# Reordering maxima, attention results and the last gate's steps in a clustered-attention and expert-layer kernel

## Chip, cores and metric

The kernel runs on one core of one Trainium2 chip. The metric is the device time of one execution in microseconds (us). Engines are named as the profile does: PE (TensorE, matmuls), PEld (its weight loads), DVE (VectorE), ACT (ScalarE), POOL (GpSimd), SP (SyncE, which issues transfers).

## What is computed

Attention in which each query sees only the keys of its own cluster, for 2 batches of 8 heads, 768 positions, 64 features; its output, 1536 tokens of 512 features, goes through a layer of 8 experts, each token to the one with the highest logit.

```
q_assign = np.argmax(einsum(q_n, c_n)); k_assign = np.argmax(einsum(k_n, c_n))
scores = np.where(q_assign == k_assign, scale * q @ k.T, -1e9)
attn = softmax(scores); x = (attn @ v) as 1536 x 512
logits = x @ w_gate; expert_idx = np.argmax(logits, axis=1)
gate_w = softmax(logits)[expert_idx]
# tokens take places in their expert's rows in order, up to capacity
y = relu(disp @ w1) @ w2; out[i] = gate_w[i] * y[expert_idx[i], pos[i]]
```

## The kernel before

The 16 heads (two batches of eight) are passes i = 0 to 15. A pass has twelve groups g. A group issues two matmuls for a 128 x 384 block of masked scores (`st_group`, L414 and L415, tile s), whose exponentials ScalarE writes (pf, L419). Before a head's scores the row maxima must be known: a maximum is a matmul (`max_tile`, L351, tile m) that VectorE reduces (mx, L358). Maxima run ahead of the scores: `ahead` takes the next one from a list of twelve per head, one behind each group, two behind the groups in `TWICE`. After a head's last one `max_chain` joins the halves (mxx, L364), and two groups later `max_rows` turns them (mtp, L390) and sends them as a row.

`hooks(i, g)` puts the rest of the work behind certain groups. At g = 2 the second values batch of pass i - 1 (`pv_batch`, L443, tile o, values times exponentials, in tiles of 128 x 64), its strips (`sum_strips`, L469, tile rsp, row sums in tiles of 128 x 32), and the evictions. At g = 5 and 6 the row sums are turned (rtp, L487) and inverted (r, L493 to L495, three steps on VectorE). At g = 8 the first values batch of pass i. At g = 11 `out_stage` (L581, tile otp): three products of the unscaled result with an identity and the gate's weights, 128 x 144 each, which `out_scale` scales at g = 2 two passes on. Odd passes also assign the clusters of a coming pair of heads: `cl_assign` ends at g = 10 with the one-hot (ohb, L259), and the next pass turns it at g = 0 (ctb, L286).

The order of each engine is what the code says (`keep`): TensorE, VectorE, ScalarE and GpSimd run their lists in order. Two tiles of PSUM serve the maxima (psM), three the scores (psS), two small results (psT), one the values (psO). `opening` holds pass 0 and the step to pass 1.

The gate (`gate`, three calls: the first batch's six blocks of 128 tokens, then the second's first three, then its last three) finds each token's expert as a one-hot (goh), counts places with matmuls (gps, L656 to L662), makes row indices (gw, gsi) and scatters the tokens (L724). The last call runs beside the first expert's first tile, in whose matmuls its steps stand; the next token rows of expert 0 can be loaded only when its scatters have landed.

Of the kernel before, what the change touches and what calls it, by code (L numbers as in the profile page):

```python
# [7 lines left out]
F32 = mybir.dt.float32  # L8
R32 = mybir.dt.float32r
BF16 = mybir.dt.bfloat16  # L10
I32 = mybir.dt.int32
AF = mybir.ActivationFunctionType
ALU = mybir.AluOpType
AX = mybir.AxisListType
# [9 lines left out]
def kernel(  # L24
# [29 lines left out]
    WARM1 = 1  # L54
    WARM2 = 12
    WARM3 = 3
    G_B0, G_B1, G_TURN, G_OUT = 8, 2, 5, 11
    TWICE = {(3, 2), (3, 3)}
    ONE = (1, 3, 5, 7)
    THREE = ONE + (2, 4, 6, 8, 9, 10, 11, 13, 14)  # L60
    HELD = (mybir.EngineType.PE, mybir.EngineType.DVE, mybir.EngineType.Activation, mybir.EngineType.Pool)
# [68 lines left out]
    def keep(ins):  # L130
        if held[0] and ins.ins.engine in HELD:
            tc.keep_in_program_order(ins)
# [315 lines left out]
                    stop=(kt == NT - 1),  # L448
                ))

    def pv_evict(h):
        oT_t[h] = work.tile([P, HALF], F32, tag="oT", name="oT", bufs=2)
        keep(nc.scalar.activation(out=oT_t[h], in_=ot.pop(h)[:, 0:HALF], func=AF.Copy))

    def sum_strips(h):
        ps = psS.tile([P, 512], F32, tag="s", name="rsp")
# [157 lines left out]
    def gate(b, t0=0, t1=NT, last=None):  # L614
        n = t1 - t0
        lg = xt[b, "l"][:, t0:t1]
        sh = [P, n, E]

        def tl(nm, last=E, dt=F32, rows=n):
            return work.tile([P, NT + 1, last], dt, tag=nm, name=nm)[:, 0:rows]  # L620

        mx = tl("gmx", 1)
        keep(nc.vector.tensor_reduce(out=mx, in_=lg, axis=AX.X, op=ALU.max))
        ex = tl("gex")
        if last:
            last()
            hl = work.tile([P, n, 1], F32, tag="held2", name="held2", bufs=1)
            keep(nc.gpsimd.tensor_copy(hl, xt[b][:, t0:t1, DM - D:DM - D + 1]))
            sm = tl("gsm", 1)
            nm = tl("gnm", 1)  # L630
            keep(nc.scalar.activation(out=nm, in_=mx, func=AF.Copy, scale=-1.0))
            for t in range(n):
                keep(nc.scalar.activation(out=ex[:, t], in_=lg[:, t], func=AF.Exp, bias=nm[:, t], accum_out=sm[:, t]))
        else:
            keep(nc.vector.tensor_tensor(out=ex, in0=lg, in1=mx.to_broadcast(sh), op=ALU.subtract))
            keep(nc.scalar.activation(out=ex, in_=ex, func=AF.Exp))
        eq = tl("geq")
        keep(nc.vector.tensor_tensor(out=eq, in0=lg, in1=mx.to_broadcast(sh), op=ALU.is_equal))
        e8 = cs[:, C_E8:C_E8 + E].rearrange("p (o c) -> p o c", o=1)
        keep(nc.vector.tensor_tensor(out=eq, in0=eq, in1=e8.to_broadcast(sh), op=ALU.mult))  # L640
        m2 = tl("gm2", 1)
        keep(nc.vector.tensor_reduce(out=m2, in_=eq, axis=AX.X, op=ALU.max))
        yield
        oh = tl("goh", E, BF16)
        keep(nc.vector.tensor_tensor(out=oh, in0=eq, in1=m2.to_broadcast(sh), op=ALU.is_equal))
        yield

        ps = psT.tile([P, 512], F32, tag="t", name="gps")
        pv = ps[:, 0:2 * n * E].rearrange("p (r t e) -> p r t e", r=2, t=n)

        def spread(x, k):
            return x.rearrange("p (o u e) -> p o u e", o=1, u=1).to_broadcast([P, 2, k, E])


        o2 = oh.rearrange("p (o t) e -> p o (t e)", o=1).to_broadcast([P, 2, n * E])
        keep(nc.tensor.matmul(out=pv.rearrange("p r t e -> p r (t e)"), lhsT=trib, rhs=o2, start=True, stop=False))  # L656
        for r in first:
            r = r.rearrange("p (u e) -> p u e", u=1).to_broadcast(sh)
            keep(nc.tensor.matmul(out=pv[:, 1], lhsT=oneb, rhs=r, start=False, stop=False))
        for t in range(n - 1):  # L660
            keep(nc.tensor.matmul(out=pv[:, :, t + 1:], lhsT=oneb, rhs=spread(oh[:, t], n - 1 - t), start=False, stop=False))
        keep(nc.tensor.matmul(out=pv, lhsT=oneb, rhs=spread(run[-1], n), start=False, stop=True))  # L662

        def prob():
            keep(nc.vector.tensor_scalar(out=sm, in0=sm, scalar1=1e-9, scalar2=None, op0=ALU.add))
            keep(nc.vector.reciprocal(out=xt[b][:, t0:t1, DM:DM + 1], in_=sm))

        if not last:
            sm = tl("gsm", 1)
            keep(nc.vector.tensor_reduce(out=sm, in_=ex, axis=AX.X, op=ALU.add))  # L670
            prob()
        w = tl("gw")
        keep(nc.vector.tensor_scalar(out=w, in0=pv[:, 0], scalar1=float(cap), scalar2=float(OOB), op0=ALU.is_ge, op1=ALU.mult))
        keep(nc.vector.tensor_tensor(out=w, in0=pv[:, 1], in1=w, op=ALU.add))
        yield
        keep(nc.vector.tensor_tensor(out=w, in0=w, in1=oh, op=ALU.mult))
        si = work.tile([P, NT, 1], I32, tag=f"gsi{b}{t0}", name="gsi", bufs=1)[:, 0:n]
        with nc.allow_low_precision(reason="a whole number and zeros"):
            keep(nc.vector.tensor_reduce(out=si, in_=w, axis=AX.X, op=ALU.add))
        if last:  # L680
            prob()
        cnew = tl("gcu", E, F32, 1)[:, 0]
        keep(nc.vector.tensor_reduce(out=cnew, in_=oh.rearrange("p t e -> p e t"), axis=AX.X, op=ALU.add))
        cum = tl("gcum", E, BF16, 1)[:, 0]
        keep(nc.vector.tensor_tensor(out=cum, in0=cnew, in1=run[-1], op=ALU.add))
        run.append(cum)
        for t in range(n):
            if t == TH:
                yield
            scatter("xd", xd, si[:, t], xt[b][:, t0 + t, :], (E * ST + 1) * P - 1)  # L690
# [66 lines left out]
    def hooks(i, g):  # L757
# [35 lines left out]
            sum_turn(i - 1)  # L793
        if i > 0 and g == G_TURN + 1:
            sum_scale(i - 1)
        if i > 0 and g == (6 if i == NH - 1 else G_OUT):
            out_stage(i - 1)
        if (i, g) in W_AT:
            w_high(W_AT.index((i, g)))
# [30 lines left out]
                pass  # L830
        if g == G_B0 and i < NH - 1:
            pv_batch(i, 0)
            p_add(i, 0)
            if i in THREE:
                p_add_rest(i, 0)
            if 0 < i < NH - 3:
                split(i + 3, 1)
                split(i + 3, 2)
            if i == H + 2:
                next(gens["g"])  # L840
            if not even and i < NH - 3:
                next(gens["c"])
# [454 lines left out]
    def opening():  # L1297
# [32 lines left out]
        split(3, 1)  # L1330
        split(3, 2)
        split(3, 3)
        sum_strips(0)
        pv_evict(0)
        ahead(2)
        ahead(2, None, psT, "t")
        ahead(1, None, psS, "s")
        sum_evict(0)

    with tc.manual_schedule():  # L1340
# [13 lines left out]
    with ExitStack():  # L1354
# [18 lines left out]

        def rest():
            last_batch(h, 1, between)
            pv_evict(h)
            sum_turn(h, psS, "s")
            yield
            last_rows(h, 1)
            last_logits(h, 1)  # L1380
            g = gate(B - 1, TH, NT, lambda: last_scale(h, 1))
            next(g)
            yield
            next(g)
            yield
            for _ in g:
                pass
            counts()
            held[0] = False
# [66 lines left out]
```

## Time and profile before

| | |
|---|---|
| median of 3 runs | 441.49 us (441.22 to 442.04) |
| profiled execution | 442.5 us, span 440.6 us |
| PE, PEld | 427.3, 340.1 us busy |
| DVE, ACT, POOL | 320.0, 275.1, 162.5 us busy |
| mean granted TensorE clock | 0.997 |

Times within the execution count from the span's start. A row of a timeline has start, duration, engine, line, operation, out<-in, and in brackets how long the engine sat idle before it and what ended that. Matmuls overlap, so where one starts says more than how long it takes.

### The profile page before, as it was taken

How to read it: one execution, taken by the hardware profiler on the slowest of the kernel's cores; microseconds unless marked ns; L12 is line 12 of the kernel's file. 1: busy time of each engine (PE TensorE's matmuls, PEld its weight loads, DVE VectorE, ACT ScalarE, POOL GpSimd, SP SyncE). 2: the span in 40 equal slices, each digit the busy share in tenths (PEclk: the TensorE clock that was granted, in tenths of full speed). 3: DMA queues.
4: the chain of work that ended last, by engine and by line, in shares of the span. 5: the costliest groups of instructions: out<-in, count | busy, mean ns of one | idle time of the engine just before them, and what ended most of it. 6: DMA issues, size and time to landing. Idle time of an engine off the chain costs nothing. (4 is left out here: it accounts for less than half of the span.)

```text
span 440.6 us, 8129 instructions
## 1 busy us (share of the span) xinstructions
PE 427.3 (97%) x2792; PEld 340.1 (77%) x2792; DVE 320.0 (73%) x674; ACT 275.1 (62%) x559; POOL 162.5 (37%) x220
## 2 busy tenths in 40 slices
PE   8999999999999999999999999999999999999993
PEld 7856767676676767766665778999999999999972
DVE  6778788787787888887866545787787878786421
ACT  6756656665666656575565544768686868686330
POOL 7974775567655664563220500001010101101010
PEclk9999999999999999999999999999999999999998
DMA  6547574581855846257122366578879797975010
GB/s 207 135 111 216 172 218 140 174 258 37 243 192 170 263 139 179 56 148 226 48 97 96 147 225 234 168 256 251 268 226 275 238 282 226 280 225 192 15 40 20
DMA packets 31224, 78.14 MB, mean 177 GB/s; under 512 B 4678, under 2 KB 5024, under 8 KB 31172
## 3 DMA queue, kind: packets, MB, share of 16 engines
q1 hardware_dynamic: 26196, 61.18, 47.2%
q0 software_dynamic: 4832, 16.15, 9.9%
q8 instruction: 29, 0.48, 0.4%
q14 instruction: 23, 0.19, 0.1%
q10 hardware_dynamic: 144, 0.16, 0.1%
HBM read 50.46 MB, written 16.76 MB: 153 GB/s over the span
## 5 line engine op out<-in xcount | busy, mean ns | idle before, releaser
L358 DVE TENSOR_REDUCE mx<-m 128x1 f32<-128x384 f32 x192 | 101.8, 552 | 36.6 <-PE m L351 36.0
L419 ACT ACTIVATE pf<-s 128x384 f32<-128x384 f32 x192 | 89.2, 494 | 44.1 <-PE s L415 34.5
L142 DVE TENSOR_TENSOR ws<-wraw,ws 128x1024 fp32r<-128x1024 f32 x64 | 78.3, 1223 | 26.5 <-ACT ws L136 26.1
L724 POOL DMA_INDIRECT out_dram<-y,row x17 | 17.9, 1053 | 166.1 <-ACT pt L1023 75.8
L414 PE MATMUL s<-W,Y 112*128 112x384 f32 (+1 forms) x192 | 73.1, 381 | 0.8 <-DVE mx L358 0.8
L1015 PE MATMUL g<-xc,ws 128*128 128x416 f32 x224 | 70.0, 373 | 1.0
L1015 PE MATMUL g<-hc,ws 128*128 128x416 f32 x224 | 69.5, 371 | 0.0
L136 ACT ACTIVATE ws<-wraw 128x1024 fp32r<-128x1024 f32 x64 | 67.1, 1048 | 0.3 <-issue 0.2
L351 PE MATMUL m<-Y,W 112*128 112x384 f32 (+1 forms) x192 | 65.8, 353 | 0.8 <-DVE mx L358 0.3
L415 PE MATMUL s<-Qs,Y 97*128 97x384 f32 (+1 forms) x192 | 65.0, 339 | 0.0
L443 PE MATMUL o<-pf,v 128*64 128x384 f32 x360 | 64.7, 494 | 0.0
L1016 PE MATMUL g<-hc,ws 128*128 128x208 f32 x224 | 57.9, 259 | 0.0
L1016 PE MATMUL g<-xc,ws 128*128 128x208 f32 x224 | 57.9, 259 | 0.0
L434 POOL TENSOR_TENSOR acc<-acc,pf 128x256 f32<-128x256 f32 x39 | 29.7, 786 | 54.4 <-DVE acc L428 40.4
L414 PEld LDWEIGHTS s<-W,Y 112*128 112x128 f32 (+1 forms) x192 | 36.3, 189 | 16.5 <-issue 13.1
L1023 ACT ACTIVATE pt<-g 128x208 f32<-128x208 f32 x84 | 27.5, 340 | 30.9 <-PE g L1016 30.4
L443 PEld LDWEIGHTS o<-pf,v 128*64 128x64 f32 x360 | 23.5, 136 | 28.3 <-issue 23.9
L1015 PEld LDWEIGHTS g<-xc,ws 128*128 128x128 f32 x224 | 42.1, 188 | 3.2 <-issue 2.8
L1016 PEld LDWEIGHTS g<-xc,ws 128*128 128x128 f32 x224 | 42.8, 191 | 0.0
L1016 PEld LDWEIGHTS g<-hc,ws 128*128 128x128 f32 x224 | 42.8, 191 | 0.0
L1015 PEld LDWEIGHTS g<-hc,ws 128*128 128x128 f32 x224 | 42.1, 188 | 0.4
L351 PEld LDWEIGHTS m<-Y,W 112*128 112x128 f32 (+1 forms) x192 | 35.7, 188 | 7.1 <-DVE mx L358 3.0
(216 smaller groups left out, 698.5 us busy)
## 6 DMA issues: line engine op xcount, KB each, us to landing
wraw<-in_w_dram SPq DMA_DIRECT2D x64, 512.0 KB
xd<-z POOLq DMA_DIRECT2D x7, 780.0 KB, 5.2
row<-xd SPq DMA_DIRECT2D x18, 260.0 KB
qv<-in_qT_dram SPq DMA_DIRECT2D x8, 384.0 KB
kv<-in_kT_dram SPq DMA_DIRECT2D x8, 384.0 KB
Y<-Y SPq DMA_DIRECT2D x32, 96.0 KB
Qs<-W SPq DMA_DIRECT2D x16, 192.0 KB
v<-in_v_dram SPq DMA_DIRECT2D x8, 384.0 KB
```

Source lines behind the costliest of these rows:

```text
L136: keep(nc.scalar.activation(out=w[:, 0], in_=raw[c], func=AF.Copy))
L142: keep(nc.vector.tensor_tensor(out=w[:, 1], in0=t, in1=w[:, 0].bitcast(F32), op=ALU.subtract))
L351: keep(nc.tensor.matmul(out=m[:, 0:HALF], lhsT=W[0:KA[h % 2], t * P:(t + 1) * P], rhs=Y1[0:KA[h % 2], j * HALF:(j + 1) * HALF], start=True ...
L358: keep(nc.vector.tensor_reduce(out=mxt[h][:, j, t:t + 1], in_=m[:, 0:HALF], axis=AX.X, op=ALU.max))
L414: keep(nc.tensor.matmul(out=s[:, 0:HALF], lhsT=Y1[0:ka, ks], rhs=W[0:ka, qs], start=True, stop=False))
L415: keep(nc.tensor.matmul(out=s[:, 0:HALF], lhsT=Y0[0:kb, ks], rhs=Qs[0:kb, qs], start=False, stop=True))
L419: keep(nc.scalar.activation(out=pt[h, u][:, slot[0], slot[1]], in_=s[:, 0:HALF], func=AF.Exp, scale=1.0 / float(D) ** 0.5))
L434: keep((nc.vector if u else nc.gpsimd).tensor_tensor(out=a[:, c:c + w], in0=a[:, c:c + w], in1=b[:, c:c + w], op=ALU.add))
L443: keep(nc.tensor.matmul(out=ot[h][j * D:(j + 1) * D, 0:HALF], lhsT=vt[h // 2][:, h % 2, kt, :], rhs=pf[:, n, j], start=(kt == 0), stop=(kt ...
L1015: nc.tensor.matmul(out=o, lhsT=w[0], rhs=x.rearrange("p o n -> p (o n)"), start=start, stop=False)
L1016: nc.tensor.matmul(out=o[:, 0:RW], lhsT=w[1], rhs=x[:, 0], start=False, stop=stop)
L1023: nc.scalar.activation(out=t, in_=o[:, RW:2 * RW], func=AF.Copy)
```

## The change

1. `opening`: of the five maxima of head 2 behind the strips and the eviction of head 0's result, four go ahead of the strips; one stays.
2. `out_stage(i - 1)` goes from behind group 11 to behind the first values batch at group 8, in passes 1 to 14. Pass 15 keeps it at group 6.
3. `TWICE` is at groups 6 and 7 of pass 3 instead of 2 and 3.
4. The gate: the one-hot times a number out of bounds (gfar) is made beside the one-hot; behind the places two steps fill the two halves of gw and one sum over sixteen makes the index, where three steps and a sum over eight did. In the last gate the maximum is taken with its sign turned, the exponentials come before the scaling of the result, and the reciprocal before the indices.
5. The last eviction of a result (`pv_evict`) is in two pieces.

```diff
-    G_B0, G_B1, G_TURN, G_OUT = 8, 2, 5, 11
-    TWICE = {(3, 2), (3, 3)}
+    G_B0, G_B1, G_TURN = 8, 2, 5
+    TWICE = {(3, 6), (3, 7)}
...
-    def pv_evict(h):
+    def pv_evict(h, cuts=(0, HALF)):
         oT_t[h] = work.tile([P, HALF], F32, tag="oT", name="oT", bufs=2)
-        keep(nc.scalar.activation(out=oT_t[h], in_=ot.pop(h)[:, 0:HALF], func=AF.Copy))
+        o = ot.pop(h)
+        for a, b in zip(cuts, cuts[1:]):
+            keep(nc.scalar.activation(out=oT_t[h][:, a:b], in_=o[:, a:b], func=AF.Copy))
...
-        keep(nc.vector.tensor_reduce(out=mx, in_=lg, axis=AX.X, op=ALU.max))
-        ex = tl("gex")
+        ex, eq = tl("gex"), tl("geq")
         if last:
+            keep(nc.vector.tensor_reduce(out=mx, in_=lg, axis=AX.X, op=ALU.max, negate=True))
+            sm = tl("gsm", 1)
+            for t in range(n):
+                keep(nc.scalar.activation(out=ex[:, t], in_=lg[:, t], func=AF.Exp, bias=mx[:, t], accum_out=sm[:, t]))
             last()
...
-            keep(nc.scalar.activation(out=nm, in_=mx, func=AF.Copy, scale=-1.0))
-            for t in range(n):
-                keep(nc.scalar.activation(out=ex[:, t], in_=lg[:, t], func=AF.Exp, bias=nm[:, t], accum_out=sm[:, t]))
+            keep(nc.vector.scalar_tensor_tensor(
+                out=eq, in0=lg, scalar=-1.0, in1=mx.to_broadcast(sh), op0=ALU.mult, op1=ALU.is_equal
+            ))
...
+        far = work.tile([P, NT, E], BF16, tag="gfar", name="gfar", bufs=1)[:, 0:n]
+        keep(nc.vector.tensor_scalar(out=far, in0=oh, scalar1=float(OOB), scalar2=None, op0=ALU.mult))
         yield
...
-            prob()
-        w = tl("gw")
-        keep(nc.vector.tensor_scalar(out=w, in0=pv[:, 0], scalar1=float(cap), scalar2=float(OOB), op0=ALU.is_ge, op1=ALU.mult))
-        keep(nc.vector.tensor_tensor(out=w, in0=pv[:, 1], in1=w, op=ALU.add))
+        prob()
+        w = work.tile([P, NT, 2 * E], F32, tag="gw", name="gw", bufs=1)[:, 0:n]
+        keep(nc.vector.scalar_tensor_tensor(
+            out=w[:, :, 0:E], in0=pv[:, 0], scalar=float(cap), in1=far, op0=ALU.is_ge, op1=ALU.mult
+        ))
+        keep(nc.vector.tensor_tensor(out=w[:, :, E:2 * E], in0=pv[:, 1], in1=oh, op=ALU.mult))
         yield
-        keep(nc.vector.tensor_tensor(out=w, in0=w, in1=oh, op=ALU.mult))
...
-        if last:
-            prob()
...
-        if i > 0 and g == (6 if i == NH - 1 else G_OUT):
+        if (i, g) == (NH - 1, 6):
             out_stage(i - 1)
...
             pv_batch(i, 0)
+            if i > 0:
+                out_stage(i - 1)
             p_add(i, 0)
...
+        ahead(2)
+        ahead(1, None, psT, "t")
+        ahead(1, None, psS, "s")
         sum_strips(0)
         pv_evict(0)
-        ahead(2)
-        ahead(2, None, psT, "t")
-        ahead(1, None, psS, "s")
+        ahead()
         sum_evict(0)
...
-            pv_evict(h)
+            pv_evict(h, (0, P, HALF))
```

What the change moves is seen in the lists of the engines. TensorE around the step from pass 0 to pass 1, before (mtp: head 1's maxima turned; rsp: strips; m: maxima of head 2; s: scores of head 1):

```order
L443 MATMUL o<-pf,v 64x384 x6
L390 MATMUL mtp<-cs,mxx 6x128
L469 MATMUL rsp<-acc,onef 32x384 x2
L469 MATMUL rsp<-pf,onef 32x384 x2
L469 MATMUL rsp<-acc,onef 32x384 x2
L469 MATMUL rsp<-pf,onef 32x384 x2
L351 MATMUL m<-Y_102,W_98 128x384 x5
L414 MATMUL s<-W_99,Y_103 128x384
```

And in the change:

```order
L443 MATMUL o<-pf,v 64x384 x6
L390 MATMUL mtp<-cs,mxx 6x128
L351 MATMUL m<-Y_102,W_98 128x384 x4
L471 MATMUL rsp<-acc,onef 32x384 x2
L471 MATMUL rsp<-pf,onef 32x384 x2
L471 MATMUL rsp<-acc,onef 32x384 x2
L471 MATMUL rsp<-pf,onef 32x384 x2
L351 MATMUL m<-Y_102,W_98 128x384
L414 MATMUL s<-W_99,Y_103 128x384
```

Four maxima stand before the strips and one behind them.

TensorE at the end of pass 3 and the start of pass 4, before (otp: results of head 2; ctb: transposes of the one-hot):

```order
L351 MATMUL m<-Y_103,W_99 128x384
L414 MATMUL s<-W_100,Y_104 128x384
L415 MATMUL s<-Qs_108,Y_112 128x384
L351 MATMUL m<-Y_103,W_99 128x384
L581 MATMUL otp<-rhb,oT 128x144 x3
L414 MATMUL s<-W_97,Y_101 128x384
L415 MATMUL s<-Qs_105,Y_109 128x384
L351 MATMUL m<-Y_103,W_99 128x384
L286 LDWEIGHTS ohb
L286 MATMUL ctb<-idb,ohb 128x128
```

And in the change, from the first values batch of pass 3 on:

```order
L390 MATMUL mtp<-cs,mxx 6x128
L443 MATMUL o<-pf,v 64x384 x6
L583 MATMUL otp<-rhb,oT 128x144 x3
L414 MATMUL s<-W_100,Y_104 128x384
L415 MATMUL s<-Qs_108,Y_112 128x384
L351 MATMUL m<-Y_103,W_99 128x384
L414 MATMUL s<-W_100,Y_104 128x384
L415 MATMUL s<-Qs_108,Y_112 128x384
```

The three products stood between the third group behind the values and the fourth, which runs ahead of the one-hot's transposes; now they stand directly behind the values, with four groups between them and those transposes.

VectorE in pass 3, from the cluster assignment of group 2 to the sum behind group 8, before (mx: a maximum's reduction; mxx: the column maximum; r: the reciprocal of the row sums):

```order
L246 TENSOR_REDUCE cmx<-ctp 128x24
L249 TENSOR_TENSOR ceq<-ctp,cmx 128x384
L358 TENSOR_REDUCE mx<-m 128x1 x3
L364 TENSOR_TENSOR mxx<-mx 128x6
L358 TENSOR_REDUCE mx<-m 128x1 x2
L493 TENSOR_SCALAR r_1021<-rtp 128x6
L494 TENSOR_TENSOR r<-rtp,r_1021 128x6
L495 RECIPROCAL r<-r 128x6
L358 TENSOR_REDUCE mx<-m 128x1 x2
L428 TENSOR_TENSOR acc<-pf 128x768
```

And in the change:

```order
L246 TENSOR_REDUCE cmx<-ctp 128x24
L249 TENSOR_TENSOR ceq<-ctp,cmx 128x384
L358 TENSOR_REDUCE mx<-m 128x1 x4
L364 TENSOR_TENSOR mxx<-mx 128x6
L358 TENSOR_REDUCE mx<-m 128x1
L495 TENSOR_SCALAR r_1013<-rtp 128x6
L496 TENSOR_TENSOR r<-rtp,r_1013 128x6
L497 RECIPROCAL r<-r 128x6
L358 TENSOR_REDUCE mx<-m 128x1 x3
L428 TENSOR_TENSOR acc<-pf 128x768
```

The column maximum comes one maximum later, between the two of group 6, and three maxima instead of two stand behind the reciprocal.

## Rows read from the trace of the kernel before

**Rows 1.** Busy time by engine, middle heads; from PE on: engine (instructions), clock, DMA share, GB/s.

```profile
50.00:150.00 100.00, 99.87 (x660) 67.74 (x657) 80.17 (x170) 61.41 (x129) 64.38 (x88) 1.00 0.62 188
```

**Rows 2.** Timeline of PE, step from pass 0 to pass 1.

```profile
31.26 0.27 PE L390 MATMUL mtp<-cs,mxx 128*6 128x128 f32 x1
...
32.89 1.14 PE L351 MATMUL m<-Y,W 112*128 112x384 f32 x5
...
35.84 0.44 PE L414 MATMUL s<-W,Y 128*128 128x384 f32 x1 [0.76 <-DVE mx L358]
```

**Rows 3.** Timeline of DVE, the same place.

```profile
33.37 3.98 DVE L358 TENSOR_REDUCE mx<-m 128x1 f32<-128x384 f32 x8 [3.04 <-PE m L351]
```

**Rows 4.** Timeline of PE, pass 2, from the first values batch to the next pass.

```profile
56.09 2.16 PE L443 MATMUL o<-pf,v 128*64 128x384 f32 x12
58.17 0.44 PE L414 MATMUL s<-W,Y 112*128 112x384 f32 x1
58.45 0.34 PE L415 MATMUL s<-Qs,Y 97*128 97x384 f32 x1
...
59.67 0.38 PE L351 MATMUL m<-Y,W 112*128 112x384 f32 x1
59.89 0.90 PE L581 MATMUL otp<-rhb,oT 128*128 128x144 f32 x6
...
60.81 0.34 PE L415 MATMUL s<-Qs,Y 128*128 128x384 f32 x1
```

**Rows 5.** Timelines of PE and DVE, pass 5, values to the one-hot's transposes.

```profile
98.02 2.16 PE L443 MATMUL o<-pf,v 128*64 128x384 f32 x12
...
101.10 0.34 PE L351 MATMUL m<-Y,W 128*128 128x384 f32 x1
...
101.95 0.55 DVE L259 TENSOR_TENSOR ohb<-ceq,cm 128x384 bf16<-128x384 bf16 x1
...
103.11 0.51 PE L286 MATMUL ctb<-idb,ohb 128*128 128x128 bf16 x6
```

**Rows 6.** Timeline of PE, pass 3, groups 3 to 8.

```profile
66.53 0.51 PE L351 MATMUL m<-Y,W 112*128 112x384 f32 x2
...
67.52 0.45 PE L351 MATMUL m<-Y,W 112*128 112x384 f32 x1
...
68.16 0.33 PE L351 MATMUL m<-Y,W 128*128 128x384 f32 x1
...
70.44 0.54 PE L443 MATMUL o<-pf,v 128*64 128x384 f32 x2
```

**Rows 7.** Timeline of DVE, pass 3, groups 4 to 8.

```profile
68.59 0.17 DVE L364 TENSOR_TENSOR mxx<-mx 128x6 f32<-128x6 f32 x1
...
69.39 0.56 DVE L358 TENSOR_REDUCE mx<-m 128x1 f32<-128x384 f32 x1 [0.16 <-PE m L351]
69.86 0.15 DVE L493 TENSOR_SCALAR r<-rtp 128x6 f32<-128x6 f32 x1
...
70.36 0.98 DVE L358 TENSOR_REDUCE mx<-m 128x1 f32<-128x384 f32 x2
```

**Rows 8.** Timeline of all engines, tail of the last gate and the wait behind it.

```profile
247.52 0.18 DVE L679 TENSOR_REDUCE gsi<-gw 128x3 int32<-128x24 f32 x1
...
247.81 0.18 DVE L666 RECIPROCAL x<-gsm 128x3 f32<-128x3 f32 x1
...
248.26 0.98 POOL L724 DMA_INDIRECT xd<-x,gsi  x1 [0.70 <-DVE gcum L685]
...
256.51 0.63 PE L885 MATMUL rtp<-cs,row 128*128 128x128 f32 x4 [0.67 <-DMA row<-xd]
```

**Rows 9.** Timeline of PE, first groups of pass 13.

```profile
199.91 0.34 PE L415 MATMUL s<-Qs,Y 128*128 128x384 f32 x1
...
202.02 0.45 PE L351 MATMUL m<-Y,W 112*128 112x384 f32 x1 [0.30 <-DVE mx L358]
```

**Rows 10.** Timeline of DVE, the one-hot in pass 0.

```profile
24.57 1.57 DVE L259 TENSOR_TENSOR ohb<-ceq,cm 128x384 bf16<-128x384 bf16 x1
```

More of the change, by code (lines that the diff above doesn't have):

```diff
@@ L628, in gate @@
             keep(nc.gpsimd.tensor_copy(hl, xt[b][:, t0:t1, DM - D:DM - D + 1]))
-            sm = tl("gsm", 1)
-            nm = tl("gnm", 1)
-            keep(nc.scalar.activation(out=nm, in_=mx, func=AF.Copy, scale=-1.0))
-            for t in range(n):
-                keep(nc.scalar.activation(out=ex[:, t], in_=lg[:, t], func=AF.Exp, bias=nm[:, t], accum_out=sm[:, t]))
+            keep(nc.vector.scalar_tensor_tensor(
+                out=eq, in0=lg, scalar=-1.0, in1=mx.to_broadcast(sh), op0=ALU.mult, op1=ALU.is_equal
+            ))
         else:
+            keep(nc.vector.tensor_reduce(out=mx, in_=lg, axis=AX.X, op=ALU.max))
             keep(nc.vector.tensor_tensor(out=ex, in0=lg, in1=mx.to_broadcast(sh), op=ALU.subtract))
             keep(nc.scalar.activation(out=ex, in_=ex, func=AF.Exp))
-        eq = tl("geq")
-        keep(nc.vector.tensor_tensor(out=eq, in0=lg, in1=mx.to_broadcast(sh), op=ALU.is_equal))
+            keep(nc.vector.tensor_tensor(out=eq, in0=lg, in1=mx.to_broadcast(sh), op=ALU.is_equal))
         e8 = cs[:, C_E8:C_E8 + E].rearrange("p (o c) -> p o c", o=1)
```

## The prediction, made before the changed kernel ran

> **What bounds the kernel now.** I read first the table of busy time by stretch, then TensorE's timeline where it pauses, then VectorE's at the same places, and last the tail of the gate. In the stretch that holds the middle heads TensorE is busy for 99.87 of 100 us at the full clock (2.4 GHz), VectorE for 80, ScalarE for 61, GpSimd for 64 [rows 1]. So a step is worth what it takes out of TensorE's stream there or puts into it; work of the other engines counts only where TensorE ends up waiting for it. Four places matter.
>
> The opening: after the first head's values the stream has one transpose (mtp, 31.26), the strips, and five maxima from 32.89; VectorE had been idle for 3.04 us and then reduces eight scores in a row, 3.98 us; the third group's scores at 35.84 wait 0.76 us for it [rows 2, 3]. The steady heads: twelve value matmuls in 2.16 us, then groups of three matmuls, and the six result matmuls (otp) between two groups [rows 4]. Head 3, which takes two extra maxima: from the pair at 66.53 to group 5's maximum at 68.16 it needs 1.63 us, where a second maximum and two groups in stride are 0.18 + 2 x 0.525 = 1.23; 0.40 is waiting for VectorE's reductions [rows 6]. The last gate: at 256.51 TensorE has stood still 0.67 us for token rows, which wait for the scatters that began at 248.26 [rows 8].
>
> **The change, part by part.** Times are those of the profiled execution: 442.5 us, its span 440.6. The median of the three runs is 441.49, 1.0 below it; the sum is made on 442.5 and the same difference taken off the median. A measurement of this kernel tells about 0.2%, 0.9 us, from no change.
>
> (1) *Opening.* Four of the five maxima go ahead of the strips. VectorE can then begin at about 31.9 instead of 33.37, and all four are reduced (0.5 us each, [rows 3]) by 34, while the strips run. The matmuls are the same, but the stream now changes between whole-array and strip tiles once more; such a change costs 0.1 (the second matmul behind it, 0.28 instead of 0.175, at 58.45) to 0.35 us. A group is three matmuls of 0.175, 0.525 us. Before, mtp at 31.26 to the first group was 2.6 us (five maxima from 32.89, the second 0.28 behind the first); now 2.8 to 2.95, and two groups later 35.1 to 35.25, where 35.84 stood [rows 2]. That is 0.6 to 0.73, and 0.1 since the matmul behind a wait loses its hidden weight load. I take **-0.75**; ends -0.9 and -0.5. ScalarE's eviction of the strips comes about 1 us later, with scores still behind it.
>
> (2) *Results behind the values.* Fifteen passes issue otp, six instructions each; that of pass 15 stays, 14 move from behind group 11 to behind the first values batch of group 8. Before: from the values' start to the second matmul behind them 58.45 - 56.09 = 2.36, and from the maximum before otp to the second matmul behind it 60.81 - 59.67 = 1.14, 3.50 in all [rows 4]. Now: values to otp 58.17 - 56.09 = 2.08, otp to the second matmul behind it 60.81 - 59.89 = 0.92, 0.05 for the second otp whose weights find no cover, and 0.35 for the two plain steps at the old place: 3.40. So -0.1 for a head. But the six odd heads 1 to 11 end in a transpose (ctb) that needs VectorE's one-hot (ohb), and the 0.6 us of otp lay between them. In head 5 ctb starts 103.11 - 98.02 = 5.09 us after the values [rows 5]. Now group 10's maximum would start 2.08 + 0.97 + 0.175 + 0.525 = 3.75 after the values; ohb starts 101.95 - 101.10 = 0.85 later, because VectorE first reduces that maximum, and takes 0.55; with 0.05 for the signal ctb can start at 5.20, not at the 4.99 that TensorE reaches: a new wait of 0.2. Behind it on TensorE stand all of the next head's groups, and ScalarE's eviction of ctb. So an odd head loses 0.1 where an even one gains 0.1: 8 x -0.1 + 6 x 0.1 = **-0.2**; ends -1.4 (ohb early) and +0.6. The result tile is held three groups longer; otp waits for no buffer, since the next user of its pair comes at the next head's start.
>
> (3) *The pair of maxima.* Head 3 takes its two extra maxima at groups 6 and 7 instead of 2 and 3. At groups 2 and 3 they cost their two steps of 0.18 and the wait of 0.40: 0.76 us. Now two tiles of PSUM serve five maxima (6, 6, 7, 7, 8) while VectorE also has the column maximum (mxx) and the three-step reciprocal (r) between them. With the gaps of rows 7, counted from group 5's maximum: the reduction of group 6's first at 1.23 (69.39 - 68.16), mxx 0.59 behind it (a reduction's 0.56 and a start), the second reduction 0.1 behind that, r 0.47 behind (69.86 - 69.39), group 7's first reduction 0.50 behind (70.36 - 69.86), which frees its tile 0.57 later: group 8's maximum cannot start before 3.46. To the values it is another 0.55, since head 4's maxima end here and their transpose (mtp) stands there too: 4.0, where it was 70.44 - 68.16 = 2.28 [rows 6, 7]. So +1.7 - 0.76 = **+0.9**; ends -0.4 (no wait at all) and +1.1. Queued behind those maxima are the scores of groups 7 and 8 and the values. Head 4's maxima row is sent two groups later, 5 us before head 4 reads it; were it late, head 4's first scores would wait.
>
> (4) *Last gate.* The third index step goes (0.2: 0.18 as the indices' own row and a start), and the sum's reciprocal, which ended at 247.99 and stood 0.27 before the scatter [rows 8], runs ahead of the index steps; the scatter can start 0.27 behind the indices. The exponentials run before the result scaling and need no negated copy, so their sums should be there in time. Together 0.29 (247.99 - 247.70) + 0.2 = 0.5 earlier than 248.26; GpSimd's own queue (two scatters, a copy) takes a little back. TensorE's wait of 0.67 shrinks by **-0.45**; ends -0.67 and 0 (the sums late, or the copy of the scaled results, which now come after the exponentials). The cut of the last eviction in two costs ScalarE one more start, beside matmuls. The count matmuls stand two matmuls earlier on TensorE; their input is earlier by as much; uncovered, 0.3.
>
> (5) *Free.* One instruction (gfar, about 0.2 as its neighbours) is added to each gate and one taken from behind the positions. In the first two gates VectorE waits for the next score anyway; the same work uncovered would be 0.2 each way. SP and GpSimd issue the same list in the same order.
>
> **Sum**: -0.75 - 0.2 + 0.9 - 0.45 = -0.5: 442.5 becomes 442.0, the median **441.0**.
>
> A row first: otp's old place costs 1.14 - 0.35 = 0.79, the new one 3.40 - 2.36 - 0.35 = 0.69; six matmuls at 0.12 (otp's 0.90 less its last matmul's tail of 0.29, over five steps) are 0.73, so I price the old place with a small stop [rows 4]. The Trainium skill, TensorEngine Tiling (Array Packing), Key Properties, says that changing the tiling mode, not just the tile, drains the engine. By that rule otp between whole-array matmuls costs no drain, and the move saves nothing; that is rival B.
>
> **The rivals.**
> A, *the pair costs no wait*: VectorE's order lets group 8's maximum through, (3) is -0.4 and not +0.9: 439.7. For it: VectorE was idle 0.16 before the reduction at 69.39, so it is not full there [rows 7]. Against: five reductions of 0.47 and r's 0.5 do not fit into the 2.3 us before the values.
> B, *otp's old place was free*: the eight heads give 0 and not -0.8: 441.8. For: the rule above. Against: the old place costs 0.06 more than its columns; but the margin is thin.
> C, *the stall behind head 12 goes as well*: from 199.91 to 202.02 TensorE takes 2.11 us, in stride 0.175 + 2 x 0.525 = 1.23, since VectorE is late [rows 9]; this is just behind otp's old place, and with otp gone there it could fall: 0.9 less, 440.1. Against: what delays VectorE there is not otp.
> D, *slower: ohb stretched by GpSimd*. In the prologue the same ohb took 1.57 us while GpSimd was adding, against 0.55 in head 5 [rows 5, 10]. It now runs 0.5 us later against GpSimd's queue. At 1.57 ctb waits 1.0 more in each of six heads: 447.1. It turns the sum to slower by over 0.2% from a stretch of 0.23 us each (1.4 / 6). Against: GpSimd was at work 64 of 100 us there and ohb kept to 0.55. The Trainium skill, GPSIMD Engine Reference, Specifications, names contention with VectorE instructions that have two SBUF inputs, which ohb has; the prologue's row agrees, head 5's does not.
>
> **How the numbers follow.** Forecast 0.45, A 0.18, B 0.14, C 0.10, D 0.13. The forecast's own bounds put a fifth of it, 0.09, below 440.6; with A and C that is 0.37 for faster. The rest of it, 0.36, and B make 0.50 for no change. D makes 0.13 for slower. The range takes in A and C below and B with the upper ends of (1) and (4) above, and leaves out D: 439.4 to 442.4.
>
> **What would show it.** Right: no wait at the third group of head 1; otp directly behind the values at about 2.1 us from their start; ctb in odd heads waiting about 0.2 for VectorE; two or three waits of 0.3 to 0.5 at head 3's groups 7 and 8; scatter 0.5 earlier against its gate and a rest of about 0.2 before the token rows' transpose. Wrong: if head 3 runs from group 5 to its values in 3 us or less, (3) is wrong and the time nears A; if ohb takes more than 0.8, D.

## The result, and the profile after

| | before | changed |
|---|---|---|
| median | 441.76 us (441.22 to 442.45) | 445.46 us (444.9 to 445.94) |
| ratio | | 1.0077, 95% interval 1.0063 to 1.009 |
| profiled execution | 442.5 us, span 440.6 | 445.84 us, span 443.9 |

The change made the kernel 3.7 us slower; 441.0 had been forecast, with 439.4 to 442.4 as its range. The prediction was wrong.

The list of what TensorE waited for in the changed kernel (engine, tile and line, what it waited for; total, times, longest) names three of the four places of the forecast, and a wait that it had put at 0.2 stands first:

```profile
PE ctb L286 <- DVE ohb L259: 2.7, 5, 0.6
...
PE s L415 <- DMA Qs<-mr: 0.7, 1, 0.7
...
PE rtp L891 <- DMA row<-xd: 0.4, 1, 0.4
PE m L351 <- DVE mx L358: 0.2, 1, 0.2
```

The transposes of the one-hot (ctb) wait for it five times; the second line, head 2's row of maxima that lands late, was in no part of the forecast. The middle heads show the loss as TensorE's busy time, 98.05 of 100 us where 99.87 stood [rows 1]:

```profile
50.00:150.00 100.00, 98.05 (x634) 66.03 (x632) 78.96 (x164) 60.83 (x126) 60.95 (x82) 1.00 0.58 180
```

To see where the time goes, I set the same score matmul, the first of group 2 of each pass, side by side in both traces and took the differences of the stretches between them:

| stretch | changed minus before, us |
|---|---|
| up to group 2 of pass 1 (opening) | -0.86 |
| pass 1 (odd, and head 2's row) | +0.49 |
| pass 3 (odd, and the pair) | +1.33 |
| passes 5, 7, 9, 11 (odd) | +0.76, +0.77, +0.75, +0.77 |
| passes 2, 4, 6, 8, 10 (even) | +0.03, +0.01, +0.03, +0.03, +0.13 |
| passes 12 and 13 | -0.40, -0.50 |
| pass 14 | +0.36 |
| last gate, from group 2 of pass 15 to the token rows | -0.41 |
| all | +3.30 |

The two places of -0.40 and -0.50 are the stall behind head 12 [rows 9]. It stands in the one profiled execution of the kernel before and in none of the thirteen others, of kernels with any of the edits or, in e10 below, with none of them; so it is no work of the change. It is more than the 0.7 by which that execution lay above its median; without it the stretches add up to 4.2, against 3.7 between the medians.

**Opening.** TensorE and VectorE around the step from pass 0 to pass 1, against [rows 2, 3]:

```profile
31.26 0.27 PE L390 MATMUL mtp<-cs,mxx 128*6 128x128 f32 x1
31.29 0.96 PE L351 MATMUL m<-Y,W 112*128 112x384 f32 x4
32.18 0.52 PE L471 MATMUL rsp<-acc,onef 128*32 128x384 f32 x2
...
33.89 0.34 PE L414 MATMUL s<-W,Y 128*128 128x384 f32 x1
...
34.98 0.34 PE L414 MATMUL s<-W,Y 128*128 128x384 f32 x1
...
31.75 1.95 DVE L358 TENSOR_REDUCE mx<-m 128x1 f32<-128x384 f32 x4 [1.42 <-PE m L351]
```

VectorE starts at 31.75 instead of 33.37, and group 2's scores follow at 34.98 instead of 35.84 with no wait. From the transpose (mtp) to the first group's scores it is 2.63, as before (2.61).

**Head 2's row.** SP sends it at 41.10, and TensorE's matmul that needs it stands still until 46.28. The kernel before sent it at 42.16 and did not wait:

```profile
41.10 0.75 SPq L393 DMA_DIRECT2D Qs<-mr  x1
...
46.28 0.44 PE L415 MATMUL s<-Qs,Y 97*128 97x384 f32 x1 [0.67 <-DMA Qs<-mr]
```

**Results in an even pass.** TensorE in pass 2, against [rows 4]:

```profile
55.71 2.16 PE L443 MATMUL o<-pf,v 128*64 128x384 f32 x12
57.79 1.00 PE L583 MATMUL otp<-rhb,oT 128*128 128x144 f32 x6
58.54 0.44 PE L414 MATMUL s<-W,Y 112*128 112x384 f32 x1
58.81 0.34 PE L415 MATMUL s<-Qs,Y 97*128 97x384 f32 x1
```

The products start 2.08 behind the values, as taken, and the second matmul behind them 1.02 later, 0.05 more than the 0.92 + 0.05 of the forecast.

**Results in an odd pass.** TensorE, VectorE and GpSimd in pass 5, against [rows 5]:

```profile
99.02 2.16 PE L443 MATMUL o<-pf,v 128*64 128x384 f32 x12
101.10 1.00 PE L583 MATMUL otp<-rhb,oT 128*128 128x144 f32 x6
...
103.92 0.34 PE L351 MATMUL m<-Y,W 128*128 128x384 f32 x1
104.87 0.51 PE L286 MATMUL ctb<-idb,ohb 128*128 128x128 bf16 x6 [0.61 <-DVE ohb L259]
...
103.68 1.14 DVE L259 TENSOR_TENSOR ohb<-ceq,cm 128x384 bf16<-128x384 bf16 x1
...
103.68 0.72 POOL L311 TENSOR_TENSOR Y<-kv,Y 64x256 fp32r<-64x256 f32 x1
```

The one-hot starts 4.66 behind the values (4.60 had been worked out) but takes 1.14 us instead of 0.55. At its start a piece of GpSimd's split (Y, L311) starts too, and takes its plain 0.72. The same piece, and the one-hot beside it, in the kernel before, where the one-hot was 0.06 ahead:

```profile
101.95 0.55 DVE L259 TENSOR_TENSOR ohb<-ceq,cm 128x384 bf16<-128x384 bf16 x1
...
102.01 1.08 POOL L311 TENSOR_TENSOR Y<-kv,Y 64x256 fp32r<-64x256 f32 x1
```

There the one-hot kept its 0.55 and the piece took 1.08. One of the two is held up, and in these rows it is the one that came second.

**Pair of maxima.** TensorE in pass 3, from group 3's maximum to the values:

```profile
65.96 0.34 PE L351 MATMUL m<-Y,W 112*128 112x384 f32 x1
...
67.01 0.39 PE L351 MATMUL m<-Y,W 112*128 112x384 f32 x1
...
69.57 0.44 PE L351 MATMUL m<-Y,W 128*128 128x384 f32 x1 [0.23 <-DVE mx L358]
...
70.98 1.83 PE L443 MATMUL o<-pf,v 128*64 128x384 f32 x10
```

From group 5's maximum to the values 70.98 - 67.01 = 3.97, where 2.28 stood; from group 3's to group 5's 1.05, where 1.63 stood [rows 6].

**Results in pass 14.** Here the exponentials, and not the one-hot, hold TensorE. Behind the third group after the values, where the products used to stand, the weights of the next scores now wait for ScalarE:

```profile
230.20 0.19 PEld L414 LDWEIGHTS s<-W,Y 128*128 128x128 f32 x1 [0.34 <-ACT pf L419]
```

In the kernel before no wait stands there: the products fill the time.

**Last gate.** VectorE and GpSimd at the indices, TensorE at the token rows, against [rows 8]:

```profile
250.77 0.20 DVE L685 TENSOR_REDUCE gsi<-gw 128x3 int32<-128x48 f32 x1
...
251.56 0.98 POOL L728 DMA_INDIRECT xd<-x,gsi  x1 [0.54 <-DVE gcum L689]
...
259.80 0.63 PE L891 MATMUL rtp<-cs,row 128*128 128x128 f32 x4 [0.38 <-DMA row<-xd]
```

From the scatter to the transpose 8.24, as before (8.25). Counted from group 2 of pass 15, the scatter starts 0.40 earlier and the transpose 0.41; TensorE's wait before it fell from 0.67 to 0.38.

### The profile page after: what moved, and what is told of

The parts are those of the page before. It is cut to its first block, busy times and chain, and to the rows that moved or that the text cites. A ratio compares the mean times of both kernels' runs of the same rounds, so it can differ in the third digit from the quotient of the medians.

```text
span 443.9 us, 8129 instructions
## 1 busy us (share of the span) xinstructions
PE 429.2 (97%) x2792; PEld 340.4 (77%) x2792; DVE 323.0 (73%) x674; ACT 275.3 (62%) x559; POOL 162.0 (36%) x220
## 5 line engine op out<-in xcount | busy, mean ns | idle before, releaser
L414 PE MATMUL s<-W,Y 112*128 112x384 f32 (+1 forms) x192 | 71.8, 374 | 0.0
```

What stands on the lines that cost most here:

```text
L414: keep(nc.tensor.matmul(out=s[:, 0:HALF], lhsT=Y1[0:ka, ks], rhs=W[0:ka, qs], start=True, stop=False))
```

## The experiments

My first theory: the odd passes lose because the one-hot now starts as a GpSimd piece starts, and waits for it. Rivals: the results themselves cost more behind the values; VectorE's own order delays the one-hot; the pair brings the loss. Each kernel ran in five rounds beside the kernel before, in three groups:

| run | median, us | before beside it | ratio, 95% interval |
|---|---|---|---|
| e1 results back | 441.96 | 441.94 | 0.9992 (0.9975 to 1.0009) |
| e2 pair back | 446.39 | 441.94 | 1.01 (1.0067 to 1.0134) |
| e3 results alone | 443.59 | 441.94 | 1.0043 (1.0024 to 1.0062) |
| e4 one-hot early | 442.06 | 441.94 | 1.0002 (0.9982 to 1.0022) |
| e5 GpSimd's pieces halved | 443.4 | 441.61 | 1.0038 (1.0026 to 1.005) |
| e6 opening alone | 441.91 | 441.61 | 1.0009 (0.999 to 1.0028) |
| e7 opening and gate | 441.36 | 441.61 | 0.9994 (0.9981 to 1.0008) |
| e8 all but the pair, one-hot early | 441.64 | 441.61 | 1.0016 (0.9989 to 1.0043) |
| e9 opening, load later | 440.8 | 441.91 | 0.9976 (0.9962 to 0.999) |
| e10 load later alone | 441.92 | 441.91 | 1.0003 (0.9992 to 1.0014) |
| e11 opening, gate, load later | 440.64 | 441.91 | 0.9971 (0.9958 to 0.9985) |
| e12 gate alone | 441.84 | 441.91 | 0.9995 (0.9981 to 1.0008) |

### e1: the changed kernel with the results back behind group 11

```diff
-        if (i, g) == (NH - 1, 6):
+        if i > 0 and g == (6 if i == NH - 1 else 11):
             out_stage(i - 1)
...
-            if i > 0:
-                out_stage(i - 1)
```

> The change with the results' products (otp) back behind group 11, all else as changed. Theory 1 (in odd passes the one-hot now starts inside a GpSimd piece, waits for the piece to end, and ctb waits for the one-hot): against the changed kernel the six odd passes give back about 0.75 us each and the even ones nothing, so about 4.2 us less, 441.2; ohb is 0.55 us long again and ctb does not wait. Theory 2 (the loss is head 3's pair and the other edits): the time stays within 1.5 us of the changed kernel, at 444 or more.

3.5 us of the loss go with this one part (theory 1 had 4.2 for it, theory 2 at most 1.5). Passes 5, 7, 9 and 11 are at 0.00 to 0.01 of the kernel before, with the one-hot at 0.546 to 0.548; pass 14 at +0.02. Its profiled execution was its longest, 446.43: head 2's row kept TensorE waiting for 3.13 us, the same wait as above. That became the second question.

```profile
49.18 0.44 PE L415 MATMUL s<-Qs,Y 97*128 97x384 f32 x1 [3.13 <-DMA Qs<-mr]
```

```profile
51.00:52.00 1.00, 1.00 (x5) 0.56 (x6) 0.60 (x2) 0.94 (x3) 0.00 (x0) 0.50 1.02 399
```

This stop cost a second time. The granted clock, 1.00 until 50 us, was 0.67, 0.50, 0.50 and 0.62 in the four us from there on (the sixth figure after the span of the row; 0.50 is the lower of the two levels, 1.2 GHz), and pass 2 took 1.41 us longer than in the kernel before, all of it in the values matmuls that ran in those four us. Behind the 1.83 us of e6 below the clock stayed at 1.00 and pass 2 lost 0.01.

### e2: the changed kernel with the pair back at groups 2 and 3

```diff
-    TWICE = {(3, 6), (3, 7)}
+    TWICE = {(3, 2), (3, 3)}
```

> The change with the two extra maxima of pass 3 back at groups 2 and 3. From the starts of the score matmuls in the two traces the pair's new place costs 0.6 us net, so 444.9 is expected. The sum before the run had 0.9 for it, 444.6. If the pair were the main loss, as theory 2 has it, 442 to 443.

In time nothing is gained, where 0.6 had been expected; of five runs the interval is wide and holds the changed kernel's own ratio. The trace says more: pass 3 is 0.55 shorter than in the changed kernel, at the pair 0.93 (3.97 - 2.28 less 1.63 - 1.05 and the 0.18 of group 2's extra maximum). The rest went to the one-hot, which in this pass takes 1.15 where it took 0.82: the pair's delay had moved it against GpSimd's pieces.

### e3: the results' move alone, on the kernel before

```diff
-        if i > 0 and g == (6 if i == NH - 1 else G_OUT):
+        if (i, g) == (NH - 1, 6):
             out_stage(i - 1)
...
             pv_batch(i, 0)
+            if i > 0:
+                out_stage(i - 1)
```

> The kernel before with the results' products moved alone. Theory 1: six odd passes lose 0.75 us each and nothing else changes, +4.5 us, 446.2, with ohb at about 1.1 us. Theory 2: no change, or a gain of some tenths.

The median is 1.65 above the kernel before, well short of theory 1's 4.5 and clear of theory 2. But the profiled execution, 442.63, was the shortest of twelve (up to 445.36), and in it an odd pass from 3 on loses only 0.14 to 0.18. VectorE, GpSimd and TensorE in its pass 5:

```profile
102.63 0.55 DVE L259 TENSOR_TENSOR ohb<-ceq,cm 128x384 bf16<-128x384 bf16 x1
...
102.66 1.11 POOL L311 TENSOR_TENSOR Y<-kv,Y 64x256 fp32r<-64x256 f32 x1
...
103.24 0.51 PE L286 MATMUL ctb<-idb,ohb 128*128 128x128 bf16 x6
```

Here the one-hot came first, by 0.023 us, and the piece was stretched to 1.11. So the order of instructions sets a tie, and hundredths of a microsecond decide it for half a microsecond a pass. That the longer executions of e3 lost the tie is likely, but no trace of one was taken.

### e4: the changed kernel with the one-hot's last steps before the odd pass's four groups

```diff
             if not even and i < NH - 3:
-                next(gens["c"])
-        if g == G_B0 + 2 and not even and i < NH - 3:
-            for _ in gens["c"]:
-                pass
+                for _ in gens["c"]:
+                    pass
```

> The change with the one-hot (ohb) right behind the column maximum of group 8 on VectorE, where VectorE idles 1.4 us, and not behind group 10's maximum. Theory 1: ohb may still wait for a GpSimd piece, but ends 2 us before ctb is reached; ctb waits no longer, about 4.3 us less than the changed kernel, 441.2. Theory 3 (ctb waits for its buffer or for the signal and not for ohb): no change, 445.5.

```profile
100.46 0.79 DVE L259 TENSOR_TENSOR ohb<-ceq,cm 128x384 bf16<-128x384 bf16 x1
...
103.29 0.51 PE L286 MATMUL ctb<-idb,ohb 128*128 128x128 bf16 x6
```

The time is 3.4 us below the changed kernel, where theory 1 had 4.3 and theory 3 nothing. The one-hot is stretched here as well, by a piece of GpSimd's sums, but ends 2 us before it is needed. Passes 5 to 11 are at -0.01 to 0.00. With the results where the change put them and no one-hot on the path, the loss is gone: it is the one-hot's, not the results'.

### e5: the changed kernel with GpSimd's split in six pieces instead of three

```diff
-    def minus(eng, out, a, b):
+    def minus(eng, out, a, b, parts=3):
...
-        w = n if eng is nc.vector else -(-n // 3)
+        w = n if eng is nc.vector else -(-n // parts)
...
-                minus(nc.gpsimd, Y0[a], d["k"][a], Y1[a])
+                minus(nc.gpsimd, Y0[a], d["k"][a], Y1[a], 6 if step == 3 else 3)
```

> The changed kernel whole, but GpSimd's third split of the K points is cut into six pieces of 128 columns instead of three of 256, so the piece that starts together with the one-hot (ohb) is half as long. Theory (ohb waits until a GpSimd piece that started just before it has ended): the wait falls from about 0.6 us to 0.4 at most, ohb takes 0.95 at most instead of 1.14, an odd pass from pass 5 on loses 0.55 or less against the kernel before instead of 0.76; about 1 to 2 us less than the changed kernel, 443.5 to 444.5. Rival (VectorE's own order delays the transposes, GpSimd has no part in it): ohb 1.14 and the odd passes +0.76 as in the changed kernel, 445.5.

```profile
103.91 0.45 POOL L311 TENSOR_TENSOR Y<-kv,Y 64x128 fp32r<-64x128 f32 x1
...
104.17 0.61 DVE L259 TENSOR_TENSOR ohb<-ceq,cm 128x384 bf16<-128x384 bf16 x1
...
104.84 0.51 PE L286 MATMUL ctb<-idb,ohb 128*128 128x128 bf16 x6
```

443.4, 2.1 below the changed kernel and just under the forecast's band. VectorE's and TensorE's orders are untouched; only GpSimd's piece differs, and the one-hot falls to 0.61, the odd passes to +0.22 to +0.24. The rival is excluded. The one-hot's durations in passes 1 to 11 of all fourteen traces follow one sum within 0.004 us: the rest, counted from its start, of the GpSimd piece that goes first, plus 0.415, and 0.548 at least.

| run, pass | rest of the piece | plus 0.415 | one-hot took | pass lost |
|---|---|---|---|---|
| e3, 5 | (came first) | | 0.548 | 0.15 |
| e5, 9 | 0.455 - 0.272 = 0.183 | 0.598 | 0.599 | 0.23 |
| changed, 3 | 0.732 - 0.331 = 0.401 | 0.816 | 0.819 | 0.40 |
| changed, 5 | 0.722 + 0.001 = 0.723 | 1.138 | 1.140 | 0.76 |

(Pass 3's 0.40 is its 1.33 less the pair's 0.93.) What the pass loses rises as the one-hot's duration does. Even the kernel before had a stretched one-hot, 0.668 in pass 1, that no transpose waited for.

Pass 0 doesn't fit a rule of one piece. The 1.57 of [rows 10] is the rest of two pieces of GpSimd's sums, up to 25.718, and 0.415: 25.718 - 24.572 + 0.415 = 1.561. The second of them started 0.43 behind the one-hot (25.004) and still went first. Why is open; in e11 the one-hot of pass 0 waited out a single piece and took 0.786.

### e6: the opening alone, on the kernel before

The edit is the change's own in `opening`.

> The kernel before with the opening's edit alone: four of head 2's maxima ahead of the strips. By the changed kernel's trace the stretch to group 2 of head 1 is 0.87 us shorter, and nothing behind it differs: 0.9 less than before, about 440.9. Rival (the time comes back later, since VectorE and ScalarE are only shifted): the same as before, 441.7.

The rival came true: no change that can be measured. The times spread from 440.64 to 444.27, and in the profiled execution head 2's second score matmul waits 1.83 us for its row:

```profile
45.57 0.43 PE L414 MATMUL s<-W,Y 112*128 112x384 f32 x1
47.83 0.44 PE L415 MATMUL s<-Qs,Y 97*128 97x384 f32 x1 [1.83 <-DMA Qs<-mr]
```

Of the eight profiles that have the opening's edit and the loads in their old place, seven show this wait: 0.2 (e7), 0.3 (e8), 0.7 (changed), 1.0 (e2), 1.5 (e5), 1.8 (e6) and 3.1 (e1); in the eighth, e4, the row was just in time (only the weight load waited, 0.17). In the kernel before and in e3, e10 and e12, which keep the old opening, it doesn't stand.

### e7: opening and gate

The changed kernel with e1's and e2's edits together.

> The changed kernel with the results back behind group 11 and the pair of maxima back at groups 2 and 3, so opening and gate alone are edited. Opening -0.9 and gate -0.45 as in the traces so far: 440.3 to 440.6, ahead of both kernels. If the stall behind head 12 also goes with this (-0.9 in all four traces of edited kernels): nearer 439.5. Rival (the 0.9 behind head 12 was a matter of one execution of the kernel before, and the gate's gain is spent in its tail): 441.0 or more.

441.36, nearer to the rival (441.0 or more) than to the forecast: the profiled execution was at 440.59 with a wait of only 0.2 for the row, but others reached 443.0. The gate's stretch is 0.46 shorter in it.

### e8: everything but the pair, one-hot early

The changed kernel with e2's and e4's edits together.

> The changed kernel with the pair of maxima back at groups 2 and 3, and the one-hot made a group pair earlier on VectorE, so that no transpose waits for it. Opening -0.9, gate -0.45, odd passes 0, even passes +0.03 each, pass 14 +0.35: 440.9. If the results in their new place are worth what I forecast (-0.1 a pass), 439.9; if the one-hot early costs VectorE a wait elsewhere, 442 or more.

441.64, between 440.9 and the 442 of its rival, with an interval on both sides of 1. The even passes 2 to 8 are at +0.02 to +0.05, pass 10 at +0.14, pass 14 at +0.34: the results gain nothing in their new place.

### e9: the opening with a later load

The load of the fourth pair's points (qv and kv, 768 KB) goes from pass 1 to pass 2, so that SP issues it behind head 2's row. On the kernel before with the opening's edit:

```diff
-        if not even and g == 0 and pi + 3 < NH // 2:
+        if not even and i > 1 and g == 0 and pi + 3 < NH // 2:
             load_pair(pi + 3)
         if (i, g) == (2, 0):
             load_v(1)
+            load_pair(3)
```

> The opening's edit alone, and the load of the fourth pair's q and k points (768 KB, used from pass 3 on) issued at pass 2 instead of pass 1, so behind head 2's row of maxima. Theory (the opening's gain runs into the transfers: head 2's row lands behind the loads under way and its second score matmul waits 0.2 to 3.1 us for it): that wait goes, the stretch from group 2 of head 1 to group 2 of head 2 is within 0.1 of the kernel before, and the 0.9 of the opening stays: 440.8 against 441.7, about 1.1 less than the opening alone. Rival (the transfers are late for another reason, or the same bytes then delay another transfer): 441.6 or more.

440.8, as forecast, 1.1 below the kernel before and under it with its whole interval. From the transpose (mtp) to group 2 of pass 1 the trace is 0.87 shorter than the kernel before (0.86 in the changed kernel), and from there to group 2 of pass 2 another 0.24 (the expectation had it within 0.1), so that the opening is worth 0.86 + 0.24 = 1.10. Busy time in the stretch before the row is needed, the DMA share second from the right: of the kernel before, the changed kernel and e9:

```profile
36.00:46.00 10.00, 9.98 (x59) 6.99 (x60) 8.58 (x20) 6.88 (x14) 4.31 (x6) 1.00 0.84 231
```

```profile
36.00:46.00 10.00, 9.60 (x61) 7.11 (x53) 8.24 (x18) 6.41 (x14) 5.38 (x8) 1.00 0.92 242
```

```profile
36.00:46.00 10.00, 9.99 (x63) 7.81 (x62) 8.80 (x19) 6.33 (x15) 6.07 (x8) 1.00 0.73 217
```

The row is 3 KB, but it travels behind 1.3 MB of loads issued from 36 us on (576 KB for rhb, 384 KB each for qv and kv). In the changed kernel SP issued the first of them 0.18 earlier than before (35.95 instead of 36.13) and the row 1.06 earlier: the loads had less time to be through, and the transfers became the end that comes last.

### e10: the later load alone, on the kernel before

> The kernel before with nothing but the load of the fourth pair moved from pass 1 to pass 2. In the profiled execution of the kernel before head 2's row was in time, so by that 0: 441.7. If the kernel before loses time to the same row in some executions: up to 0.3 less in the median and a narrower spread of its times.

No difference, as expected of the trace: without the opening's edit the row was in time. Its profile also settles the stall behind head 12. TensorE at the start of pass 13, against [rows 9]:

```profile
199.85 0.34 PE L415 MATMUL s<-Qs,Y 128*128 128x384 f32 x1
...
201.07 0.38 PE L351 MATMUL m<-Y,W 112*128 112x384 f32 x1
```

1.22 from the score to the third maximum, in stride, where the one execution of the kernel before took 2.11. Nothing is edited there.

### e11: opening, gate and the later load

e7 with e9's load.

> Opening and gate edited, results and pair where they were, and the load of the fourth pair at pass 2. Opening -0.9, gate -0.45, nothing given back at head 2: 440.3 to 440.5, faster than both kernels by over 0.2%. Rival (the gate's or the opening's gain is lost elsewhere): 441.2 or more.

440.64, 1.3 below the kernel before, the fastest of the study and ahead of both kernels: ratio 0.9971 (0.9958 to 0.9985).

### e12: the gate alone, on the kernel before

> The kernel before with the gate's edit and the cut eviction alone. By the traces of the edited kernels the wait before the token rows is 0.44 to 0.5 shorter: 441.2 against 441.7. Rival (the gate's gain needs the earlier clock of the rest, or is within the noise of the rows' landing): 441.7. And the 0.9 behind head 12: gone here as in all edited kernels, or there as in the one profile of the kernel before, which says whether it belongs to any edit at all.

441.84, not to be told from the kernel before by its median, as the rival had it. The scatter starts 0.40 to 0.45 earlier, counted from group 2 of pass 15, in all nine traces with the gate's edit, and within 0.02 of the kernel before in the four without. But from the scatter to the token rows it is 8.12 to 8.39 over the traces, and e12 has the 8.39: its stretch to the token rows is 0.30 shorter, and 0.41 to 0.49 in the changed kernel, e7 and e11. Against e9, e11's median is 0.16 lower. The gate gains some tenths, less than a measurement can tell. The stall behind head 12 is absent here too.

## Why the prediction was wrong, point by point

**(2) Results behind the values: the step that failed.** It read "ohb starts ... 0.85 later ..., and takes 0.55". The start was right to 0.06; the 0.55 was not, and with it fell the wait of 0.2 and the 0.1 for an odd head. The 0.55 [rows 5] was the duration of an instruction that had come 0.06 us ahead of GpSimd's piece. Moved by 0.7 us against GpSimd's queue it met the next piece at its start, waited that piece out, and took 1.14. Passes 5 to 11 lost 4 x 0.76 = 3.05 where 0.4 had been forecast: most of the miss. At 0.55 the step holds: e3 measured 0.15 for the forecast 0.1.

This is the mechanism of rival D, at a little more than half its price (a stretch of 0.59 and not of 1.02: the 1.57 was two pieces) and with a chance of 0.13. What spoke against it, "GpSimd was at work 64 of 100 us there and ohb kept to 0.55", was the weak argument: a busy share says nothing about who comes first. The trace before had the answer in two rows: the piece at 102.01 took 1.08 beside a one-hot at 101.95, so the two did exclude each other in head 5, with GpSimd as the loser. Laid out at the new start, 98.02 + 4.60 = 102.62, the pieces at their plain pitch of 0.69 (three sums and the start of the first split, 99.93 to 102.01) put the next start at 102.70: a tie within 0.1. D's "0.5 us later against GpSimd's queue" hid that: by the prediction's own figures it is 4.60 - (101.95 - 98.02) = 0.67, almost one pitch.

The Trainium skill, SBUF — State Buffer, section "SBUF: two separate sides", states it outright: the pair of ports that VectorE and GpSimd share is an exclusive lock, held by whoever starts first for the whole instruction, while the other one blocks; VectorE needs it in instructions with two SBUF inputs, against a GpSimd instruction that reads SBUF, as the pieces do. The traces of passes 1 to 11 agree, in both directions: 0.55 to 1.14 for the one-hot, 0.72 to 1.08 and 1.11 for the piece. By the records' starts pass 0 does not: there a piece that started later went first. The prediction cited only the page that names the contention, and asked how busy GpSimd was instead of who starts first.

The even heads were to gain 0.1 each and lost 0.01 to 0.03 (pass 10: 0.13, where the gate's count matmuls already stood behind the values): the old place was free but for hundredths. Here rival B was right, and with it the rule it rested on (the Trainium skill, TensorEngine Tiling (Array Packing), Key Properties: a changed mode drains, a changed tile does not); the 0.06 of rows 4 that I priced against it came back as 0.05 behind the new place. Pass 14 lost 0.36 for a reason of its own that I had not looked for: at the old place TensorE must wait 0.34 for ScalarE's exponentials, a wait that the products had covered. Of the 0.77 that they cost behind the values, taking them from the old place gives back 0.41, where in pass 4 it gives back nearly all of 0.71.

**(1) Opening.** At the third group the gain was 0.86 for the forecast 0.75, and e9 shows 1.10 in all. The forecast's price for one more change between tiles did not show: 2.63 from mtp to the first group, where it had 2.8 to 2.95. The failed step is what was left unsaid, what is late next: head 2's row behind the loads. In the changed kernel pass 1 gives back 0.49 where e9 gains a further 0.24, so the row costs 0.7. The one-hot of that pass, 0.81 long, has no part in it: it ended at 46.19, before the row let TensorE go on at 46.28. Alone (e6) the edit is worth nothing that can be measured, and with the loads out of the way (e9) 1.1.

**(3) Pair.** Forecast +0.9, with 4.0 from group 5's maximum to the values; measured 3.97 and +0.93. The working held step by step. A part of it returned, since the later values moved that pass's one-hot to another phase of GpSimd (0.82 instead of 1.15).

**(4) Last gate.** Forecast -0.45, trace -0.41, the scatter's own time unchanged. Of its signs, the scatter was to come 0.5 earlier and came 0.40, and the rest of the wait was to be about 0.2 and was 0.38: TensorE itself reached the place 0.12 earlier.

**(5) Free.** With the gate's edit alone (e12), beside the first gate, no stretch of passes 9 to 12 up to the stall differs by over 0.03: nothing came to light.

**The rivals.** A fell with (3); C's stall did go, but with or without the edits, so it was not the move's. Had the one-hot kept 0.55 and the row been in time, the traces' terms would give 6 x 0.15 + 0.23 + 0.36 = 1.5 for the passes, -1.1, +0.9 and -0.4, so +0.9: at the edge of what can be told from no change, and still above the forecast, for the even heads and pass 14. The chances were not badly shared between gains; too little of them lay on the one mechanism with a large price.

## What to carry to other kernels

When a VectorE instruction with two SBUF inputs is moved on the way to a wait, lay GpSimd's instructions out beside its new start: in passes 1 to 11 here whoever came first kept its time and the other waited the rest of it out (in pass 0 the rest of two pieces), so a duration read at one phase doesn't hold at another. The cheap cures are to make the instruction early enough that its stretching is hidden (e4), or to cut GpSimd's pieces, which cures a part (e5). And a gain just behind a burst of loads is worth only what the next small transfer allows: look for the row that must arrive next, and issue the large loads behind it (e9).

## What the hardware showed that I had not expected

How finely the tie is decided. In e2 a piece whose record starts 0.013 us behind the one-hot's still went first (one-hot 1.153), and in e3 one that starts 0.015 behind lost (one-hot 0.548, piece 1.114). So the order of two records this close doesn't tell who went first. The two outcomes differ by 0.6 us a pass, and each repeats in every odd pass from 3 on, since GpSimd's run of pieces starts at a fixed distance behind VectorE's sum.

And how far a small row's landing varies under full queues: e1, e6 and e7 issue the same instructions up to that point, and the wait for head 2's row was 3.1, 1.8 and 0.2 us in their profiled executions. A part is when the loads were issued: the first of them at 37.11 in e1 and 36.98 in e6, behind a transfer that took SP 1.48 and 1.42 us to issue, and at 36.14 in e7. But e8, with the same 4.28 us as e6 from the first load to the row, waited 0.3 us; the rest is open. The times of e6 spread over 3.6 us, those of the kernel before beside it over 2.2.
